# A later branch and an earlier conversion in a fused attention, expert and Fourier-mixing kernel

## The chip, the cores and the metric

The kernel runs on one core of one Trainium2 chip. The metric is the device time of one execution in microseconds (us); smaller is better. The engines are PE (TensorE, matrix products; PEld is its weight load), DVE (VectorE), ACT (ScalarE), POOL (GpSimd) and SP (SyncE, which here only issues DMA transfers).

## What is computed

Three layers follow each other on 4 sequences of 576 rows with 512 channels.

```python
x = attention_with_decay(q, k, v)                  # 8 heads, no softmax
for b, s:                                          # 8 experts, one per row
    e = argmax(logits[b, s]) or the expert of the row before
    out[b, s] = p[e] * (relu(x[b, s] @ w1[e]) @ w2[e])
u  = x + real(fft(fft(x, axis=1), axis=2))         # x: the experts' output
un = (u - mean(u)) / sqrt(var(u) + 1e-06)
y  = u + relu(un @ w_ch1) @ w_ch2                  # 512 -> 2048 -> 512
```

## The kernel before

Every large matrix product is made of three float16 products: each float32 operand is split into a high part (names with `h`) and a low part (names with `l`), and the products are high·high, high·low and low·high. A weight matrix is worked on in pieces of 128x1024. One piece takes the largest absolute value of each partition (`absmax`, L234 on ACT or L236 on DVE), then for a whole matrix one common scale: `peak` (L250 to L255) makes a diagonal matrix `diag` on DVE, `spread` (L260) multiplies it with ones on PE so that each partition sees all maxima, DVE takes the maximum (L261), `scale` (L266, L269) makes the factor `ws`, and `split` makes the high part on ACT (L276) and the low part on DVE (L281).

The channel weights arrive as 64-bit floats. DVE builds the 32-bit floats out of the integer words with five operations for a tile of 128x512: three in `convert_first` (L294, L296, L298), two in `convert_second` (L303, L306). Of the 16 pieces of the two channel matrices (`jobs`), 14 are converted during the experts. The last two, pieces 6 and 7 of the second matrix `w2`, are converted in the channel part by `convert` (L1679), half a piece at a time, and stored to DRAM.

The experts (`moe`) go one after another. For each, `products` (L807) makes the first layer in 8 steps f, ACT and POOL take relu and split (L818, L820, L822), `outputs` makes the second layer (L834, 24 products), ACT scales the result into `y` (L846), and POOL scatters its rows to `x2` in DRAM with an indirect DMA (L848). The last expert has 128 rows; its remaining 160 rows (`late`) and one more group run through `late.hidden`, f = 0 to 3 at the end of `moe` and f = 4 to 7 at the start of `channels`; there the low part `hidl` is made on DVE.

`overflow` holds a loop for experts with more rows than planned. Its branch (L2085, `If(most > 0)`) is met once by every engine and the loop isn't entered with these inputs. In the kernel before, it stands between two hand-ordered schedules: the part of the program ahead of it is arranged by a scheduler, and everything behind it runs in the order in which the code is written. The scheduler mixes nine of the last expert's 24 output products between the steps of its first layer, puts 22 of the 24 products of the late rows' f = 0 and 1 ahead of the branch on PE, and on POOL puts the branch ahead of the scatter.

Behind the branch, `channels` loads the rows of the first of 4 batches from `x2` (`tr.load(0)`, SP, L1191 and L1157), finishes the late rows and makes the Fourier transform of batch 0: `even` and `odd` fold the rows on DVE (L1204 to L1221: tiles `xe`, `xo`, `fee`, `foo`), `twice` adds and subtracts folds (L1227, L1228), `down` is the transform along the rows on PE (L1248, from `fee` and `foo`), `adds` and `sums` put the parts together (L1340, L1343).

Then comes the first channel layer of batch 0, a loop over f = 0 to 15. In each f, PE makes 12 products of 128x512 (L1613, banks `g`, three of them in turn), ACT takes the relu (`gr`, L1809) and a cast (L1810), and DVE the low part (`hd`, L1811). Two generators add one step in each f: `more` (`tr.steps(1)`, from f = 7 on) is the transform of batch 1, and `left` (`rest()`) is the work on weights: it ends the first matrix in f = 0 to 3, converts piece 6 in f = 4 to 7 and piece 7 in f = 8 to 11, and then comes to the common scale (`peak`, `spread`, `scale`) and the splits of the second matrix. Ahead of `down(0)` of batch 1, 22 products whose result isn't used (L1578) are put on PE. The second channel layer (L1827) follows, and then the same for the other batches.

Of the kernel before, what the change touches and what calls it, by code (L numbers as in the profile page):

```python
# [9 lines left out]
FP32 = mybir.dt.float32  # L10
FP16 = mybir.dt.float16
BF16 = mybir.dt.bfloat16
I32 = mybir.dt.int32
# [39 lines left out]
DONE = 14  # L53
# [237 lines left out]

def convert_first(V, r, t):

    V.tensor_scalar(out=t, in0=r[:, :, 1], scalar1=0x7FFFFFFF, scalar2=None, op0=ALU.bitwise_and)  # L294
    f = t.bitcast(FP32)
    V.tensor_scalar(out=f, in0=f, scalar1=TINY, scalar2=None, op0=ALU.max)  # L296

    V.tensor_scalar(out=t, in0=t, scalar1=3, scalar2=0x3FFFFFF8, op0=ALU.logical_shift_left, op1=ALU.bitwise_and)  # L298


def convert_second(V, r, t):

    V.scalar_tensor_tensor(  # L303
        out=t, in0=r[:, :, 1], scalar=-0x40000000, in1=t, op0=ALU.bitwise_and, op1=ALU.bitwise_or
    )
    V.scalar_tensor_tensor(  # L306
        out=t, in0=r[:, :, 0], scalar=29, in1=t, op0=ALU.logical_shift_right, op1=ALU.bitwise_or
    )


class Doubles:
# [13 lines left out]
    def first(self, j):  # L325
        t = self.t[j] = self.pool.tile([128, 1024], I32, tag="d", name="d", bufs=2)
        convert_first(self.nc.vector, self.raw[j], t)
# [533 lines left out]
class Late:  # L861
# [18 lines left out]
    def outputs(self, bank):  # L880
# [15 lines left out]
        first=1.4,  # L896
# [9 lines left out]
        first=0.3,  # L906
        second=3.6,
        store=6.9,
        raw=0.5,
# [58 lines left out]
def moe(octx, tc, nc, A, xs, x2, rows_in, rows_out, pieces, weights, who, conv, low, start, beyond, z, hid0, mt0, wst, small):  # L968
# [82 lines left out]
    def out(w, hid, mt, fs, t, n, do, amid=None):  # L1051
        y = lambda: wk.tile([128, 512], FP32, tag="y", name="y", bufs=3)
        ps = p2.tile([128, 512], FP32, tag="ps2", name="ps2")
        leave = outputs(nc, ps, y, x2, rows_out, w, hid, mt[:, t, 0:1], fs[:, t : t + 1], t, n, amid)
        for job in do:
            job()
        leave()
# [43 lines left out]
    first = [[] for _ in range(8)]  # L1101
# [6 lines left out]
    for e in range(E):  # L1108
        w, n = weights(e), CAPS[e] if e < E - 1 else HEAD
        if e == E - 1:  # L1110
            pieces.more = None
        xt, mt = X.pop(e)
        if e > 0 and e + 1 < E:
            fetch(e + 1)
        tiles = (n + 127) // 128

        todo = halves(weights, conv, 2 * e, 8) if e else first
        hid = wk.tile([128, 2, 8, n], FP16, tag="hid", name="hid", padded_shape=[128, 2, 8, CAP])
        hid = [hid[:, x] for x in range(2)]
        for f in range(8):  # L1120
            ps = p1.tile([128, CAP], FP32, tag="ps1", name="ps1")[:, 0:n]
            products(nc, ps, *w.dst, xt, f)
            for do in todo[f]:
                do()
            if f == 4 and e + 2 < E:
                pad(e + 2)
            r = wk.tile([128, CAP], FP32, tag="r", name="r", bufs=3)[:, 0:n]
            for _ in relu(nc, nc.gpsimd, ps, r, hid, f):
                pass
        fs = factors(w, mt, tiles + (end.n + 127) // 128 if e == E - 1 else tiles)  # L1130
        if e == E - 1:
            end.fs = fs
        for i, m in ((n // 128, n % 128), (tiles + end.n // 128, end.n % 128 if e == E - 1 else 0)):
            if m:

                to, k = mt[:, i, 0:1], 128 // m
                nc.vector.tensor_scalar(out=to, in0=to, scalar1=float(k), scalar2=side[k], op0=ALU.mult, op1=ALU.add)
        if e == E - 1:
            mx.close()
            yield  # L1140
        todo = halves(weights, conv, 2 * e + 1, tiles) if e else [[sizes]]
        for t in range(tiles):

            amid = partial(weights(e + 1).spread, 0, lambda: bank()[:, 0:128]) if e and t == 0 else None
            out(w, hid, mt, fs, t, n, todo[t], amid)
    end.hidden(range(LATE), bank, lambda: wk.tile([128, CAP], FP32, tag="r", name="r", bufs=3))
    ctx.close()
    yield end
# [12 lines left out]
class Transform:  # L1161
# [299 lines left out]
    def place(self, b, i):  # L1461

        t, y = i % 3, i // 3
        k0, n = TL[t]
        p0 = 1 if y and t < 2 else 0
        at = b * S + k0 + (n if y else 0)
        return t, y, p0, n, slice(at, at + n - p0)
# [62 lines left out]
def channels(ctx, tc, nc, A, w1, w2, un, u, out, tr, wst, idn, late, jobs):  # L1530
# [4 lines left out]
    cp = pool(name="gc", bufs=1)  # L1535
# [16 lines left out]
    h1, l1 = w1.dst  # L1552
    h2, l2 = w2.dst
    w2.shared.bank = lambda: p2.tile([128, 512], FP32, tag="g2", name="peak")[:, 0:128]
    tr.load(0)
    nc.sync.dma_start(out=orow, in_=A["orow"])
    turn = [0]
# [12 lines left out]
    some, final = late.outputs(bank)  # L1570
    leave = some()
    z = [bank() for _ in range(5)]
    V = nc.vector

    def still(n, ps):

# [29 lines left out]
    xt = [room().rearrange("p (k n) -> p k n", k=4) for _ in range(2)]  # L1606

    def first(f, ps, xt, steps=range(3)):

        for i in steps:  # L1610
            m, x = ((h1, 0), (l1, 0), (h1, 1))[i]
            for k in range(4):
                nc.tensor.matmul(  # L1613
                    out=ps,
                    lhsT=m[:, k + 4 * (f // 8), 128 * (f % 8) : 128 * (f % 8) + 128],
                    rhs=xt[x][:, k, :],
                    start=(k == 0 and i == 0),
                    stop=(k == 3 and i == 2),
                )

    def weave(*gs):
        gs = list(gs)
        while gs:
            gs = [g for g in gs if next(g, gs) is None]
# [7 lines left out]
    rest = bank()  # L1632
    idle(IDLE[0])
    adds = [tr.add(0, t, *ps[t]) for t in range(3)]
    weave(adds[0])
    tr.sums(0, 0)
    next(adds[1])
    rates = [tr.rate(0, [0]), tr.rate(0, [1, 2])]
    next(rates[0])
# [11 lines left out]
    weave(turns[0])  # L1651
    weave(turns[3])

    half = [[x[:, :, c] for x in xt] for c in (slice(0, 255), slice(255, 512))]
    ahead = [bank() for _ in range(4)]
    ahead = [ahead[i] for i in (0, 3, 1, 2)]
    place = lambda f, c: ahead[f][:, 0:255] if c == 0 else ahead[f][:, 255:512]
    for f in range(3):
        first(f, place(f, 0), half[0], range(2))
    norms = {i: tr.scaled(0, i, e) for i, e in ((1, nc.scalar), (4, V), (2, V))}  # L1660
    turns = [tr.turned(0, i, norms[i], xt, bank()) for i in (1, 4, 2)]
    weave(*turns)
    for f in range(4):
        first(f, place(f, 0), half[0], range(2 if f < 3 else 0, 3))
    for f in range(4):
        first(f, place(f, 1), half[1])

    def last():

# [9 lines left out]

    def convert(j):  # L1680

        V = nc.vector
        t = w2.pieces[j] = wst.tile([128, 1024], FP32, tag="wst", name="wst")
        for i in range(2):
            raw = wst.tile([128, 512, 2], I32, tag="wst", name="raw")
            nc.sync.dma_start(out=raw, in_=jobs[8 + j][0][:, i])
            convert_first(V, raw, t[:, 512 * i : 512 * i + 512].bitcast(I32))
            yield
            convert_second(V, raw, t[:, 512 * i : 512 * i + 512].bitcast(I32))
            yield  # L1690
        w2.absmax(j)
# [121 lines left out]
    for _ in left:  # L1813
        pass
    V.scalar_tensor_tensor(
        out=fs[:, 0:1], in0=w1.inv[:, 0:1], scalar=2.0**-10 / C2, in1=w2.inv[:, 0:1], op0=ALU.mult, op1=ALU.mult
# [6 lines left out]
    for t in range(4):  # L1823
        ps = p2.tile([128, 512], FP32, tag="g2", name="g2")
        for f in range(16):
            for i, (m, x) in enumerate(((h2, 0), (h2, 1), (l2, 0))):
                nc.tensor.matmul(  # L1827
                    out=ps,
# [30 lines left out]
    for r0 in range(512, NT, 256):  # L1859
        xt = X.pop(r0)  # L1860
        xt = xt[:, 0:4], xt[:, 4:8]
        j = (r0 - 512) // 256
# [12 lines left out]
        for f in range(8):  # L1875
# [36 lines left out]
        steps = [  # L1912
            (0, "d2", ((slice(0, 4, 2), 1),)),
            (1, "d1", ((slice(1, 4, 2), 1),)),
            (2, "e1", ((slice(0, 4, 3), 1),)),
            (3, "w22", ((0, 2), (1, 1))),
            (5, "e3", ((0, 1),)),
            (4, "w11", ((2, 1), (3, 2))),
            (6, "e2", ((3, 1),)),
        ]  # L1920
        if j == 0:

            steps = steps[3:6] + steps[2:3] + steps[6:] + steps[:2]
# [12 lines left out]
        def place(i):  # L1936
            q, tag = (p2, "g2") if i % 3 else (p1, "g1")
            return q.tile([128, 512], FP32, tag=tag, name=tag)[:, 0:256]
# [195 lines left out]
def fused_kernel(tc, A, out, stop=None):  # L2134
    nc = tc.nc
    with ExitStack() as ctx:
        xs = tc.dram_tile([(E + 1) * REG, XW], FP16, name="xs")
        x2 = tc.dram_tile([NT, 512], FP32, name="x2")
# [3 lines left out]
        with tc.manual_schedule():  # L2142
            wp = ctx.enter_context(tc.tile_pool(name="wp", bufs=1))
            wst = ctx.enter_context(tc.tile_pool(name="wst", bufs=8))
# [4 lines left out]
            bufs = [  # L2149
                (wp.tile([128, 8, 1024], FP16, name=f"wh{j}"), wp.tile([128, 8, 1024], FP16, name=f"wl{j}"))  # L2150
                for j in range(2)
            ]
# [21 lines left out]
            jobs = []  # L2174
# [72 lines left out]
            idn, n_i, who, low, start, beyond = attention(keep, tc, nc, A, xs, rows_in, hook, beside, after, z, weights(0), bufs[1], hid0, mt0)  # L2247
# [10 lines left out]
            next(steps)  # L2258
            for t, n in zip(tables, ("f_cs", "f_sn", "f_cd", "f_sd")):
                nc.sync.dma_start(out=t.rearrange("p a b -> p (a b)"), in_=A[n])  # L2260
        overflow(tc, nc, A, xs, x2, idn, n_i)
        with tc.manual_schedule():
            late = next(steps)
            c2x.close()
            tr = Transform(ctx, tc, nc, x2, un, u, rows_out, tables)
            channels(ctx, tc, nc, A, c1, c2, un, u, out, tr, wst, idn, late, jobs)
# [46 lines left out]
```

## Time and profile before

| what | value |
|---|---|
| time, median of 3 runs | 809.13 us (806.35 to 814.45) |
| profiled execution, its own time | 809.86 us |
| its span | 808.1 us |
| mean granted TensorE clock | 0.98 of full speed |
| PE busy | 741.5 us, 92% |
| DVE busy | 604.2 us, 75% |
| ACT busy | 418.9 us, 52% |
| POOL busy | 189.6 us, 23% |

The span is the time from the first to the last instruction in the trace; the execution's own time has 1.8 us more. In the timelines each row is a group of equal instructions: start, time from start to the end of the last, engine, line and operation, and in brackets how long the engine had been idle and what released it. A granted clock of 1.00 is TensorE at 2.4 GHz, 0.50 at 1.2 GHz.

### The profile page before, as it was taken

To read this page: it belongs to the slowest core of one execution; us is meant where nothing else is said; L and a number is where in the kernel's file an instruction comes from. 1 tells how busy PE (TensorE), PEld (TensorE's weight loads), DVE (VectorE), ACT (ScalarE), POOL (GpSimd) and SP (SyncE) were. 2 spreads that over 40 slices of the span, in tenths; PEclk is the share of its full clock that TensorE was granted. 3 is DMA by queue.
4 is the path that set the end of the run, shared out by engine and by line. 5 is a ranking of instruction groups with operands and counts; after the bars stand their busy time and mean duration, and the time that the engine had idled before them with its cause. 6 is when DMAs were issued, how large, how long until landed. Compare 5 with 4: busy or idle time off the path is not lost. (4 is left out here: it accounts for less than half of the span.)

```text
span 808.1 us, 17327 instructions
## 1 busy us (share of the span) xinstructions
PE 741.5 (92%) x6571; PEld 552.4 (68%) x6571; DVE 604.2 (75%) x1390; ACT 418.9 (52%) x857; POOL 189.6 (23%) x289
## 2 busy tenths in 40 slices
PE   8898898899899898789998999989889999999996
PEld 5687775546556555566644547868778888888885
DVE  3578988877898898857787986978958495737362
ACT  1356654778788787864744643515423361504140
POOL 3566442544355245322100002010010101010101
PEclk9999999999999999999998999999999999999998
DMA  9998349889899889932256357620380016110000
GB/s 294 348 302 312 108 131 306 226 296 374 312 280 322 319 248 310 351 110 91 84 175 236 127 192 204 188 68 2 112 198 2 27 53 171 53 33 21 27 2 27
DMA packets 91932, 142.30 MB, mean 176 GB/s; under 512 B 48116, under 2 KB 49017, under 8 KB 90814
## 3 DMA queue, kind: packets, MB, share of 16 engines
q1 hardware_dynamic: 87246, 126.78, 48.9%
q0 software_dynamic: 4592, 14.31, 4.6%
q8 instruction: 54, 0.88, 0.4%
q14 instruction: 40, 0.33, 0.1%
HBM read 97.55 MB, written 35.12 MB: 164 GB/s over the span
## 5 line engine op out<-in xcount | busy, mean ns | idle before, releaser
L1613 PE MATMUL g<-gxt,wh 128*128 128x256 f16 (+1 forms) x992 | 143.5, 285 | 3.6 <-DMA gxt<-un 3.4
L1927 PEld LDWEIGHTS <-hd 128*128 128x128 f16 x1176 | 114.7, 98 | 26.6 <-issue 6.4
L1613 PEld LDWEIGHTS <-wh 128*128 128x128 f16 x1056 | 103.1, 98 | 29.7 <-issue 8.4
L281 DVE SCALAR_TENSOR_TENSOR wl<-wst,ws,wh 128x1024 f16<-128x1024 f32 (+1 forms) x82 | 102.9, 1288 | 20.4 <-ACT wh L276 20.1
L1787 POOL DMA_INDIRECT out<-u,orow x18 | 19.1, 1064 | 391.2 <-DVE u L1956 293.3
L276 ACT ACTIVATE wh<-wst,ws 128x1024 f16<-128x1024 f32 x80 | 88.8, 1141 | 35.5 <-DVE ws L269 35.5
L807 PE MATMUL ps<-xt,wh 128*128 128x320 f16 (+4 forms) x544 | 81.3, 292 | 6.6 <-DMA xt<-xs 3.6
L807 PEld LDWEIGHTS <-wh 128*128 128x128 f16 x640 | 59.4, 103 | 38.7 <-issue 20.8
L834 PE MATMUL ps<-wh,hid 128*128 128x512 f16 (+2 forms) x528 | 84.2, 302 | 0.5 <-POOL hid L822 0.5
L1927 PE MATMUL g<-wh,hd 128*128 128x256 f16 x448 | 78.3, 273 | 2.9 <-DVE s L1898 1.6
L1613 PE MATMUL g<-gxt,wl 128*128 128x256 f16 (+1 forms) x496 | 80.5, 285 | 0.0
L1898 DVE SCALAR_TENSOR_TENSOR s<-g,r 128x256 f32<-128x256 f32 x168 | 53.1, 370 | 31.3 <-ACT hd L1892 30.5
L834 PEld LDWEIGHTS <-hid 128*128 128x128 f16 (+2 forms) x792 | 46.3, 100 | 42.5 <-issue 2.5
L822 POOL TENSOR_TENSOR hid<-r,hid 128x320 f16<-128x320 f32 (+3 forms) x64 | 64.0, 1011 | 41.4 <-ACT hid L820 40.8
L1956 DVE SCALAR_TENSOR_TENSOR u<-g,ffs,u 128x256 f32<-128x256 f32 (+1 forms) x63 | 34.1, 567 | 49.3 <-PE g L1927 48.7
L1891 ACT ACTIVATE r<-g 128x256 f32<-128x256 f32 x56 | 21.2, 379 | 92.8 <-PE g L1613 86.8
L1927 PE MATMUL g<-e,hd 128*128 128x256 f16 x504 | 61.2, 276 | 5.4 <-DVE u L1956 4.4
L1871 ACT ACTIVATE hd<-s 128x640 f16<-128x640 f32 x56 | 41.3, 737 | 46.8 <-DVE s L1898 46.8
L1927 PE MATMUL g<-wl,hd 128*128 128x256 f16 x224 | 61.1, 273 | 0.0
L1613 PEld LDWEIGHTS <-wl 128*128 128x128 f16 x528 | 51.8, 98 | 11.8 <-issue 1.1
L234 ACT ACTIVATE wh<-wst 128x1024 bf16<-128x1024 f32 x51 | 53.5, 1050 | 9.1 <-DMA wst<-in_moe_w 5.1
L834 PE MATMUL ps<-wl,hid 128*128 128x512 f16 (+2 forms) x264 | 56.3, 302 | 0.0
(303 smaller groups left out, 1352.3 us busy)
## 6 DMA issues: line engine op xcount, KB each, us to landing
wst<-in_moe_w SPq DMA_DIRECT2D x64, 512.0 KB
raw<-in_ch SPq DMA_DIRECT2D x14, 1024.0 KB
qk<-in_qkv SPq DMA_DIRECT2D x18, 512.0 KB
vk<-in_qkv SPq DMA_DIRECT2D x16, 512.0 KB
pair<-ch SPq DMA_DIRECT2D x32, 256.0 KB
ch<-d SPq DMA_DIRECT2D x14, 512.0 KB
wst<-ch SPq DMA_DIRECT2D x14, 512.0 KB
u<-u SPq DMA_DIRECT2D x9, 512.0 KB
```

Source lines behind the costliest of these rows:

```text
L234: self.nc.scalar.activation(out=x, in_=t, func=ACTF.Abs, accum_out=self.am[:, j : j + 1])
L276: self.nc.scalar.activation(out=self.dst[0][:, j, :], in_=self.pieces[j], func=ACTF.Copy, scale=self.by(j))
L281: self.nc.vector.scalar_tensor_tensor(out=l[:, j, c], in0=self.pieces[j][:, c], scalar=self.by(j), in1=h[:, j, c], op0=ALU.mult, op1=ALU.s ...
L807: nc.tensor.matmul(out=ps, lhsT=m[:, k, 128 * f : 128 * f + 128], rhs=xt[:, x + k, :], start=(k == 0 and i == 0), stop=(k == 3 and i == 2),)
L822: e.tensor_tensor(out=l[:, f, :], in0=r, in1=h[:, f, :], op=ALU.subtract)
L834: nc.tensor.matmul(out=ps[r * j : r * j + r, 0:d], lhsT=hid[x][:, f, 128 * t : 128 * t + r], rhs=m[:, 4 + f // 2, c : c + d], start=(f == ...
L1613: nc.tensor.matmul(out=ps, lhsT=m[:, k + 4 * (f // 8), 128 * (f % 8) : 128 * (f % 8) + 128], rhs=xt[x][:, k, :], start=(k == 0 and i == 0) ...
L1871: nc.scalar.activation(out=hd[:, 0, 2:7], in_=s, func=ACTF.Copy, scale=C2 / 2)
L1891: nc.scalar.activation(out=r, in_=p[:, 1:3], func=ACTF.Relu)
L1898: V.scalar_tensor_tensor(out=d, in0=x, scalar=0.0, in1=y, op0=ALU.max, op1=op)
L1927: nc.tensor.matmul(out=ps, lhsT=hid[k][:, y, x, :], rhs=E[w][m][k], start=(k == 0 and m == y == 0), stop=(k == 7 and y == 1),)
L1956: V.scalar_tensor_tensor(out=y, in0=p, scalar=fs[:, c : c + 1], in1=y, op0=ALU.mult, op1=ALU.add)
```

## The change

There are two edits. The first puts a `yield` into `moe` behind the loop over the last expert's output tiles, and the branch of `overflow` there, inside the hand-ordered schedule: the last expert's products and scatter stand ahead of it, all of the late rows' products behind it. The second takes piece 6 of the second matrix out of the loop: its two halves are loaded right behind the branch (`raws`), ahead of the rows of batch 0. Half 0 is converted behind the low parts of the late rows' f = 0 to 3. Half 1 is converted around `adds[0]` of batch 0's transform. `convert(6)` then only takes `absmax`.

```diff
@@ moe
             out(w, hid, mt, fs, t, n, todo[t], amid)
+    yield
     end.hidden(range(LATE), bank, ...)
@@ channels
+    first_t = wst.tile([128, 1024], FP32, tag="wst", name="wst")
+    raws = [cp.tile([128, 512, 2], I32, tag="gxt", name="raw", bufs=2) for _ in range(2)]
+    for i in range(2):
+        nc.sync.dma_start(out=raws[i], in_=jobs[DONE][0][:, i])
+    half = lambda i: (V, raws[i], first_t[:, 512 * i : 512 * i + 512].bitcast(I32))
+    V = nc.vector
+    convert_first(*half(0))
+    convert_second(*half(0))
     tr.load(0)
@@
     adds = [tr.add(0, t, *ps[t]) for t in range(3)]
+    convert_first(*half(1))
     weave(adds[0])
     tr.sums(0, 0)
+    convert_second(*half(1))
@@ convert(j)
+        if j == DONE - 8:
+            w2.pieces[j] = first_t
+            w2.absmax(j)
+            return
@@ fused_kernel
-        overflow(tc, nc, A, xs, x2, idn, n_i)
-        with tc.manual_schedule():
+            next(steps)
+            overflow(tc, nc, A, xs, x2, idn, n_i)
             late = next(steps)
```

On SP, behind the branch, this stood before (`fxy` holds the rows of batch 0, `x_58` is `x2`):

```order
L2085 UNCONDITIONAL_BRANCH x2
L1191 DMA fxy_6438<-x_58 128x512
L1157 DMA fxy_6438<-x_58 112x512
L1157 DMA fxy_6438<-x_58 15x512
L1191 DMA fxy_6439<-x_58 128x512
```

And this stands there now:

```order
L2098 UNCONDITIONAL_BRANCH
L1559 DMA raw<-in_ch 128x1024 x2
L1192 DMA fxy_6435<-x_58 128x512
L1158 DMA fxy_6435<-x_58 112x512
L1158 DMA fxy_6435<-x_58 15x512
L1192 DMA fxy_6436<-x_58 128x512
```

Two loads of half a piece each have come ahead of the first load of rows.

On DVE, in the loop over f, this stood before around the common scale of the second matrix (`hd` at the top is that of f = 12):

```order
L303 SCALAR_TENSOR_TENSOR wst<-raw,wst 128x512
L306 SCALAR_TENSOR_TENSOR wst<-raw,wst 128x512
L1811 TENSOR_TENSOR hd<-gr,hd 128x512
L236 TENSOR_REDUCE am<-wst 128x1
L250 TENSOR_REDUCE wm<-am 128x1
L251 TENSOR_SCALAR wm<-wm 128x1
L255 TENSOR_SCALAR diag<-idn,wm 128x128
L1811 TENSOR_TENSOR hd<-gr,hd 128x512
L261 TENSOR_REDUCE wg<-peak 128x1
```

And this stands there now (the folds at the top are those of batch 1's first 128 rows, which follow `hd` of f = 7; `hd` at the end is that of f = 8):

```order
L1211 TENSOR_TENSOR fee_6438<-xe 128x128
L1218 TENSOR_TENSOR xo<-fxy_6435 128x512
L1220 TENSOR_TENSOR xo<-xo 128x255
L1221 TENSOR_TENSOR foo_6442<-xo 128x127
L1222 TENSOR_TENSOR foo_6442<-xo 128x128
L236 TENSOR_REDUCE am<-wst 128x1
L250 TENSOR_REDUCE wm<-am 128x1
L251 TENSOR_SCALAR wm<-wm 128x1
L255 TENSOR_SCALAR diag<-idn,wm 128x128
L1824 TENSOR_TENSOR hd<-gr,hd 128x512
```

The common scale has moved four steps of f ahead, to right behind the first folds of batch 1, with no conversion ahead of it any more but that of piece 7.

On PE, this stood before around `spread` (the products of the two `g` banks belong to f = 13 and 14):

```order
L1613 MATMUL g_7371<-gxt,wh_75 128x512
L1248 MATMUL zps<-f_cs,fee_6444 128x145
L1248 MATMUL zps<-f_cs,fee_6442 128x145
L1248 MATMUL zps<-f_cs,fee_6443 128x290
L260 LDWEIGHTS onesb
L260 MATMUL peak<-diag,onesb 128x128
L1613 LDWEIGHTS wh_75
L1613 MATMUL g_7404<-gxt,wh_75 128x512
```

And this stands there now (the banks are those of f = 9 and 10):

```order
L1621 MATMUL g_7245<-gxt,wh_75 128x512
L260 LDWEIGHTS onesb
L260 MATMUL peak<-diag,onesb 128x128
L1621 LDWEIGHTS wh_75
L1621 MATMUL g_7282<-gxt,wh_75 128x512
```

The product of `spread` now stands between the first layer's steps f = 9 and f = 10, ahead of every `down` of batch 1.

## Rows read from the trace of the kernel before

**Rows 1.** Timeline of PE: start, us, engine, line, operation, tiles, count [idle before].
```profile
352.35 0.96 PE L807 MATMUL ps<-xt,wh 128*128 128x160 f16 x6 [2.94 <-PEq L2085]
...
359.04 0.38 PE L834 MATMUL bank<-wh,hidh 128*128 128x512 f16 x1
```

**Rows 2.** Instructions of the branch, L2085: count, shortest/median/longest in ns, first start.
```profile
L2085 PEldq COMPARE_BRANCH  x1: 3352/3352/3352, 348.6 to 348.6; - x1
```

**Rows 3.** Timeline of ACT, POOL and SP from the last scatter on.
```profile
348.51 0.67 ACT L846 ACTIVATE y<-ps,fs 128x512 f32<-128x512 f32 x1
...
350.91 0.99 POOL L848 DMA_INDIRECT x<-y,mt  x1 [5.26 <-issue]
...
355.30 0.34 SPq L1191 DMA_DIRECT2D fxy<-x  x1
```

**Rows 4.** Timeline of DVE from the late rows to the sums of batch 0.
```profile
359.93 0.32 DVE L822 TENSOR_TENSOR hidl<-r,hidh 128x160 f16<-128x160 f32 x1 [0.51 <-ACT hidh L820]
360.18 0.69 DVE L1204 TENSOR_TENSOR xe<-fxy 128x512 f32<-128x512 f32 x1
...
375.08 0.42 DVE L1340 TENSOR_TENSOR fxy<-fxy,bank 128x256 f32<-128x256 f32 x1 [2.19 <-ACT own L1338]
...
378.63 0.42 DVE L1340 TENSOR_TENSOR fxy<-fxy,bank 128x256 f32<-128x256 f32 x1 [1.84 <-ACT own L1338]
```

**Rows 5.** Timeline of PE in the transform of batch 0.
```profile
369.22 1.04 PE L1248 MATMUL bank<-f_sn,foo 128*128 128x145 f32 x4 [0.25 <-DVE foo L1227]
```

**Rows 6.** Timeline of SP and DVE: a conversion in the loop, as it was.
```profile
401.31 0.83 SPq L1686 DMA_DIRECT2D raw<-in_ch  x2
...
405.72 0.43 DVE L294 TENSOR_SCALAR wst<-raw 128x512 int32<-128x512 int32 x1 [1.85 <-DMA raw<-in_ch]
...
407.59 0.68 DVE L303 SCALAR_TENSOR_TENSOR wst<-raw,wst 128x512 int32<-128x512 int32 x1
```

**Rows 7.** Windows: us, busy PE PEld DVE ACT POOL, granted clock, DMA share, GB/s.
```profile
357.00:357.50 0.50, 0.50 (x10) 0.50 (x8) 0.06 (x1) 0.38 (x2) 0.00 (x0) 1.00 0.98 373
```

**Rows 8.** Timeline of PE in the loop over f.
```profile
403.00 1.89 PE L1613 MATMUL g<-gxt,wh 128*128 128x512 f16 x8
...
419.69 4.91 PE L1578 MATMUL zps<-wh 128*128 128x512 f16 x22
427.58 2.30 PE L1248 MATMUL zps<-f_cs,fee 128*128 128x145 f32 x6 [2.98 <-DVE fee L1227]
429.68 1.91 PE L1613 MATMUL g<-gxt,wh 128*128 128x512 f16 x4
...
434.49 1.15 PE L1248 MATMUL zps<-f_cs,fee 128*128 128x145 f32 x6
```

**Rows 9.** Timeline of DVE in the loop over f.
```profile
412.71 0.68 DVE L1811 TENSOR_TENSOR hd<-gr,hd 128x512 f16<-128x512 f32 x1
...
416.49 0.42 DVE L294 TENSOR_SCALAR wst<-raw 128x512 int32<-128x512 int32 x1
...
430.63 1.21 DVE L236 TENSOR_REDUCE am<-wst 128x1 f32<-128x1024 f32 x1
...
432.26 0.29 DVE L255 TENSOR_SCALAR diag<-idn,wm 128x128 bf16<-128x128 f32 x1
...
435.73 0.29 DVE L261 TENSOR_REDUCE wg<-peak 128x1 f32<-128x128 f32 x1 [2.58 <-PE peak L260]
```

**Rows 10.** Timeline of ACT in the loop over f.
```profile
412.83 1.06 ACT L234 ACTIVATE wh<-wst 128x1024 bf16<-128x1024 f32 x1 [3.81 <-DVE wst L306]
...
436.44 2.19 ACT L276 ACTIVATE wh<-wst,ws 128x1024 f16<-128x1024 f32 x2 [0.31 <-DVE ws L269]
438.53 0.58 ACT L1809 ACTIVATE gr<-g 128x512 f32<-128x512 f32 x1
```

**Rows 11.** Window behind PE's idle in the loop (columns as in rows 7).
```profile
433.50:434.50 1.00, 1.00 (x5) 0.51 (x4) 0.00 (x0) 0.00 (x0) 0.00 (x0) 0.67 0.94 307
```

**Rows 12.** Timeline of PE at a later idle.
```profile
592.50 0.60 PE L1613 MATMUL g<-gxt,wh 128*128 128x256 f16 x4 [3.03 <-DMA gxt<-un]
```

More of the change, by code (lines that the diff above doesn't have):

```diff
@@ L1572, in channels @@
     z = [bank() for _ in range(5)]
-    V = nc.vector
     def still(n, ps):
@@ L1652, in channels @@
     weave(turns[3])
-    half = [[x[:, :, c] for x in xt] for c in (slice(0, 255), slice(255, 512))]
+    parts_of = [[x[:, :, c] for x in xt] for c in (slice(0, 255), slice(255, 512))]
     ahead = [bank() for _ in range(4)]
@@ L1658, in channels @@
     for f in range(3):
-        first(f, place(f, 0), half[0], range(2))
+        first(f, place(f, 0), parts_of[0], range(2))
     norms = {i: tr.scaled(0, i, e) for i, e in ((1, nc.scalar), (4, V), (2, V))}
@@ L1663, in channels @@
     for f in range(4):
-        first(f, place(f, 0), half[0], range(2 if f < 3 else 0, 3))
+        first(f, place(f, 0), parts_of[0], range(2 if f < 3 else 0, 3))
     for f in range(4):
-        first(f, place(f, 1), half[1])
+        first(f, place(f, 1), parts_of[1])
     def last():
@@ L1680, in convert @@
     def convert(j):
-        V = nc.vector
+        if j == DONE - 8:
+            w2.pieces[j] = first_t
+            w2.absmax(j)
+            return
         t = w2.pieces[j] = wst.tile([128, 1024], FP32, tag="wst", name="wst")
```

## The prediction

> **What bounds the kernel now.** I read the page's busy shares first: PE works for 92% of the span, so time is lost or won where PE stands idle or at the low clock, and only there. The timeline of PE shows two such places beside the edits. At the branch it idles 2.94 us [rows 1], and the branch instruction itself lasts 3352 ns [rows 2]. In the loop over f it idles 2.98 us ahead of `down(0)` of batch 1, waiting for DVE's `fee` [rows 8]; behind that the granted clock is 0.67 as late as 433.5 to 434.5 [rows 11], and the same six `down` products take 2.30 us there against 1.15 us at 434.49 [rows 8]. The timeline of DVE says what PE waits for: from `xe` at 360.18 [rows 4] DVE folds batch 0 with hardly a gap, and PE follows it in idles such as 0.25 us for `foo` [rows 5]. In the loop DVE carries the conversions, the folds and `hd` one behind the other. So both edits are judged by DVE's queue, and by what PE's order makes of it.
>
> **The branch and the scatter.** The same products, relus and one scatter are issued, in another order. On POOL the scatter starts at 350.91, 1.73 us behind `y`, which ends at 349.18 (348.51 + 0.67) [rows 3], since the branch's instructions stand ahead of it. Now it stands ahead of them. But `y` itself moves back a little, as nine of its 24 products no longer fill gaps of the first layer; I put `y` at +0.1 to +0.8 and the scatter at 350.2 to 351.0, and take 350.5. SP issues the first load of rows 4.4 us behind the scatter's start (355.30 - 350.91) [rows 3]; its first transfer is then possible at 354.9. On PE, 22 products that stood ahead of the branch come behind it. Before, 74 products took from 352.35 to 359.04, 6.7 us [rows 1], part of it at half speed. 96 products from a start between 349.7 and 352 end at 356.4 to 359.8. This is near 359.04, and PE isn't what the folds wait for, so I count nothing. Were DVE not in the way, this end could cost 0.8 us or win 2.6 us.
>
> **The two new loads and half 0.** SP's first transfers are now the two halves of piece 6, 0.52 MB each, and the rows come two issues later, each 0.42 us (0.83 for two) [rows 6]: 355.7 for 354.9, against 355.30 before. DVE can't begin `xe` until half 0 is converted, since its five operations stand ahead of the last four `hidl` in program order. They cost three times 0.43 and twice 0.68, 2.65 us [rows 6]. When does half 0 land? The row nearest to it is the loop's own load: issued at 401.31, used at 405.72, 4.4 us, with other transfers under way [rows 6]. At the rate of a full queue, 373 GB/s [rows 7], 0.52 MB take 1.4 us behind a start of about 1 us, 2.5 us in all. The queues are nearly empty here, so I take the lower end: landed at 357.4, converted at 360.1, four `hidl` of 0.32 [rows 4] to 361.4, `xe` at 361.5 instead of 360.18: +1.3 us. The upper end is 359.3 and +3.1. The low end is +0.3, if the data lands at 356.4, about when DVE is done with the first four `hidl`.
>
> The Trainium skill (DMA: Bandwidth & Descriptors, the table of two cost components) gives a transfer about 2.0 us fixed plus its bytes over 436 GB/s, as an estimate 3.2 us here. By it half 0 would land at 358.1 and the term would be +2.0; rows 6 alone, with its 4.4 us, stands above it.
>
> **Half 1.** Three operations (1.3 us) go ahead of `adds[0]` and two (1.4 us) behind `sums(0,0)`. DVE idles 2.19 and 1.84 us in just these two places, ending at 375.08 and 378.63, while ACT works on `own` [rows 4]. These idles cover them; without the cover half 1 would cost 2.65 us. I count nothing.
>
> **The loop over f.** The edit takes 5.3 us of conversion off DVE. But the order shows where the time goes: `rest()` runs one step in each f, and with `convert(6)` reduced to `absmax`, everything behind it comes four steps earlier, the common scale too. Nothing else on DVE ahead of f = 8 becomes shorter, because piece 7's conversion now stands in f = 4 to 7 where piece 6's stood. ACT takes `absmax` of piece 6 at f = 4, 1.06 us [rows 10], ahead of the relu of f = 4; PE loses about 1 us of its lead in f = 7. The row at 403.00 holds the last four products of f = 6 and the first four of f = 7; twelve products of 0.216 us (22 take 4.75 and the tail of the last) make 2.59 us a step, so f = 7 began at 403.86 and f = 9 now ends at 403.86 + 1.0 + 3 x 2.59 = 412.6 on the old scale [rows 8]. Its next product is `spread`, and that needs `diag`. On DVE, `hd` of f = 7 ends at 413.4 (412.71 + 0.68), the folds of batch 1's first rows run until 416.49, and then come L236 to `diag`, which took from 430.63 to 432.55, 1.92 us [rows 9]: 418.4. PE stands idle for 5.8 us where it did not before.
>
> From there: `hd` of f = 8 to 418.9, the second folds (3.2 us, as the first) to 422.1, L261, L266 and L269 to 422.8 [rows 9]. ACT then makes the high parts of two pieces, 2.19 us, ahead of the relu of f = 9 with 0.58 [rows 10]: 425.6. PE makes f = 10 and 11 from 418.45, 5.2 us at full clock, but f = 12 needs the bank of f = 9, so not before 425.65. Then 2.6 us for f = 12, 4.75 us for the 22 filler products [rows 8], 0.95 us for `down(0)` (1.15 with the tail), whose `fee` I put at 432.7, behind the folds of the last 66 rows, two more low parts and two `hd`, so that its idle of 2.98 us is gone, and 2.6 us for f = 13: `down(1)` at 436.55. Before it stood at 434.49 [rows 8]: **+2.05 us**. This holds if the low clock behind the idle costs no more than the 2.0 us by which f = 11 ends ahead of the bank. If it costs what it cost behind 427.58 (1.15 us for `down` and 2.2 us for f = 13, whose twelve products take from 429.68 to 434.49 instead of 2.59), f = 12 starts at 427.0 and `down(1)` at 437.9: +3.4. Behind it, f = 13 to 15 have only `hd` on DVE, and PE was dense there anyway, so nothing comes back. If ACT and PE come out of f = 8 with more lead than I give them, the idle is longer and its end the same.
>
> The Trainium skill (TensorE: Matmul & The Clock Gate, Part 1) says that an idle PE falls back to half its rate. By rows 11 it did so here after 2.98 us; by that rule the 5.8 us would leave the low clock behind them too, and the sum would be the larger one, +4.7, if that stretch is as long as the one that rows 8 shows.
>
> **The sum.** +1.3 for half 0 and +2.05 for the early scale: +3.35. The profiled execution is 809.86 us with a span of 808.1; it becomes 813.2. The median of the three runs is 0.7 lower, so I predict **812.5 us**. The bounds of the two terms (+0.3 to +3.1, +2.05 to +3.4) give 811.5 to 815.6, on the median. Runs of before lie between 806.35 and 814.45.
>
> **The rivals.** *The loop wins what it gives up* (faster). If `diag` is ready before PE ends f = 9, at 412.6, there is no new idle, while the idle of 2.98 and the low clock behind it (3.3 us) are gone: -6.3 + 1.3, 804.1 us. DVE would have to be 5.8 us earlier. For it speaks that 5.3 us of DVE work has left the loop; against it that this work left from behind f = 8, and `diag` stands behind a full piece of conversion and a fold. It decides at the start of L236: 410.7 or before. Were the branch's idle and its half speed shortened too, 801 is as far as it goes.
>
> *The loads hold up the front and the clock stays low* (slower). Half 0 takes 4.4 us as in the loop, +3.1, the rows behind two loads of 0.52 MB come later still, and PE is at half clock for as long as behind 427.58, +3.4: +6.5, 815.6 us. For it speak rows 6 and rows 11; against it that the queues are nearly empty at 355.
>
> *The delay is swallowed later.* PE has idles behind the loop, such as 3.03 us at 592.50 for a load of `gxt` [rows 12]. If what they wait for were issued by an engine with slack, a delay of 3 us would shorten them: 809 to 810 us. Against it: that load follows DVE work which follows PE's own products, so it comes later with them.
>
> **How the numbers follow.** The forecast (811 to 814) has 0.5, the slow front and clock 0.2, the swallowed delay 0.2, the win in the loop 0.1. The range of 8 in 10 reaches from the runs near the swallowed delay, 806.5, to the slow case with the runs' scatter, 818.5; about 0.1 lies on either side. A measurement of this kernel can tell about 1% from no change, that is 801.0 and 817.2. Faster than that asks for the win in the loop and a gain at the branch: 0.06. Slower asks for the slow case and more: 0.14. Within 1%: 0.80.
>
> **What would show it.** Right: PE idle for about 6 us ahead of the product of `spread`, released by `diag`; no idle ahead of `down(0)` of batch 1; L294 of half 0 released by the load of `raw`; `xe` at about 361.5; the scatter before 351. Wrong: `diag` on DVE earlier than PE's end of f = 9, a `raw` that lands before the fourth `hidl`, or later idles of PE that shrink by as much as the loop lost.

## The result, and the profile after

The changed kernel takes 818.21 us (median of 10 runs, 815.03 to 819.38); the kernel before, run beside it, 812.09 us (10 runs, 806.35 to 814.65; the three runs shown ahead of the prediction are among them). The ratio is 1.0069, 95% interval 1.0045 to 1.0092: **slower by 0.7%**, some 5.6 us by the ratio and 6.1 by the medians. A second measurement, of 4 runs, gave 1.0118 (1.0084 to 1.0152) with a median of 821.12. The first median lies within the range of 806.5 to 818.5, 0.3 us below its upper end; the second lies above it. The size that was predicted, 3.35 us, was too small.

The profiled execution has a span of 816.9 us for 808.1. The first view is the timeline of PE of the changed kernel, from the branch to the second channel layer.

```profile
350.37 0.44 PE L807 MATMUL ps<-xt,wh 128*128 128x160 f16 x4 [1.26 <-PEq L2098]
...
367.69 1.47 PE L1249 MATMUL bank<-f_cs,fee 128*128 128x145 f32 x8 [1.74 <-DVE fee L1228]
370.47 3.14 PE L1249 MATMUL bank<-f_cs,fee 66*128 66x290 f32 x10 [1.31 <-DVE fee L1210]
...
426.22 0.29 PE L260 MATMUL peak<-diag,onesb 128*128 128x128 bf16 x1 [6.35 <-DVE diag L255]
426.30 1.92 PE L1621 MATMUL g<-gxt,wh 128*128 128x512 f16 x4
...
435.87 4.91 PE L1586 MATMUL zps<-wh 128*128 128x512 f16 x22
440.62 1.15 PE L1249 MATMUL zps<-f_cs,fee 128*128 128x145 f32 x6
...
444.19 1.15 PE L1249 MATMUL zps<-f_cs,fee 128*128 128x145 f32 x6
```

Three things answer to [rows 1, 8]. The idle at the branch is 1.26 us instead of 2.94. The idle of 2.98 ahead of `down(0)` of batch 1 is gone, the six products take 1.15 us and not 2.30. But the product of `spread` waits 6.35 us for its diagonal, and there are two new idles in batch 0's transform, 1.74 and 1.31 us, in which PE waits for DVE's folds (`fee`).

The timelines of DVE, POOL and SP of the changed kernel answer to [rows 3, 4]:

```profile
350.31 1.50 POOL L848 DMA_INDIRECT x<-y,mt  x1 [4.39 <-ACT y L846]
354.17 1.77 SPq L1559 DMA_DIRECT2D raw<-in_ch  x2
356.25 0.33 SPq L1192 DMA_DIRECT2D fxy<-x  x1
...
358.58 0.43 DVE L294 TENSOR_SCALAR wst<-raw 128x512 int32<-128x512 int32 x1 [2.89 <-DMA raw<-in_ch]
...
361.31 0.79 DVE L822 TENSOR_TENSOR hidl<-r,hidh 128x160 f16<-128x160 f32 x3
362.41 0.33 DVE L822 TENSOR_TENSOR hidl<-r,hidh 128x160 f16<-128x160 f32 x1 [0.31 <-ACT hidh L820]
363.90 0.69 DVE L1205 TENSOR_TENSOR xe<-fxy 128x512 f32<-128x512 f32 x1 [1.17 <-DMA orow<-in_orow]
...
382.37 0.42 DVE L1341 TENSOR_TENSOR fxy<-fxy,bank 128x256 f32<-128x256 f32 x1 [4.64 <-ACT own L1339]
```

The scatter is earlier, half 0 is converted from 358.58 on, and the folds start at 363.90 instead of 360.18. DVE is through with half 0 and the low parts at 362.74 and then waits 1.17 us for a load (the profile names `orow`, a small load issued right behind the rows; in a second profile the idle is 0.41 us and the load is that of the rows). The transform then takes longer than it did: `adds` starts 18.5 us behind the folds, where it was 14.9 [rows 4]. The windows of the changed kernel show why (us, busy time of PE, PEld, DVE, ACT and POOL, granted clock, DMA share, GB/s):

```profile
366.00:376.00 10.00, 7.00 (x27) 4.73 (x28) 9.52 (x25) 2.65 (x10) 1.06 (x2) 0.76 0.39 145
376.00:386.00 10.00, 10.00 (x65) 9.52 (x63) 4.64 (x13) 3.22 (x11) 1.27 (x1) 0.73 0.16 54
```

In the kernel before, in a second profile of it (the ratio of its runs to the others of this kernel was 0.9988, 0.9956 to 1.0019), the same windows read

```profile
366.00:376.00 10.00, 9.63 (x62) 6.89 (x60) 8.05 (x22) 3.09 (x12) 1.06 (x2) 1.00 0.29 99
376.00:386.00 10.00, 8.90 (x156) 7.45 (x155) 6.79 (x25) 6.43 (x19) 4.68 (x4) 1.00 0.01 2
```

PE worked through batch 0's transform at 2.4 GHz before; now, from 371.2 on, 0.7 us behind the second idle, it stands at 1.2 GHz until 381.

To compare profiles, the span is cut where the same work begins. The time up to the end of `y` of the last expert varies between profiles by several us (348.2 to 355.1) and is left out. "y" is that end, "folds" the start of the first `xe`, "f = 4" the first 128x512 product of the channel layer's loop, "second layer" the first product of L1827 or what it became. All are read from the timelines, in us.

| profile | y to folds | folds to f = 4 | f = 4 to second layer | rest | y to end |
|---|---|---|---|---|---|
| before | 11.0 | 35.9 | 46.3 | 365.7 | 458.9 |
| before, second profile | 11.3 | 35.7 | 45.5 | 364.6 | 457.2 |
| changed | 13.9 | 39.5 | 48.7 | 364.8 | 466.9 |
| changed, second profile | 12.9 | 39.3 | 49.2 | 365.3 | 466.7 |
| branch alone | 10.1 | 40.0 | 45.2 | 364.7 | 460.0 |
| conversion alone | 13.7 | 37.8 | 48.7 | 365.0 | 465.2 |
| late scale | 13.7 | 39.1 | 41.0 | 365.5 | 459.3 |
| fill | 14.9 | 35.8 | 48.6 | 363.9 | 463.1 |
| late scale and fill | 12.9 | 35.8 | 41.1 | 365.3 | 455.0 |
| rows first | 10.0 | 38.8 | 40.7 | 364.8 | 454.2 |
| half 0 later | 12.8 | 40.5 | 49.5 | 365.6 | 468.3 |
| one half | 10.6 | 36.5 | 45.8 | 364.3 | 457.2 |
| half 1 at f = 1 | 10.7 | 36.6 | 41.0 | 364.3 | 452.6 |
| the same, old branch | 11.1 | 37.7 | 40.8 | 365.1 | 454.7 |

The change costs 2.2 us up to the folds (13.4 for 11.2, means of two profiles each), 3.6 in batch 0's transform (39.4 for 35.8), 3.1 in the loop (49.0 for 45.9), and nothing behind it. That is 8.7 us in the profiles; the two ratios give 5.6 and 9.6.

### The profile page after: what moved, and what is told of

It reads as the page before. It is cut to its first block, busy times and chain, and to the rows that moved or that the text cites. A ratio compares the mean times of both kernels' runs of the same rounds, so it can differ in the third digit from the quotient of the medians.

```text
span 816.9 us, 17330 instructions
## 1 busy us (share of the span) xinstructions
PE 743.2 (91%) x6571; PEld 553.7 (68%) x6571; DVE 605.7 (74%) x1390; ACT 419.3 (51%) x857; POOL 191.5 (23%) x289
## 5 line engine op out<-in xcount | busy, mean ns | idle before, releaser
L1969 DVE SCALAR_TENSOR_TENSOR u<-g,ffs,u 128x256 f32<-128x256 f32 (+1 forms) x63 | 34.1, 569 | 49.3 <-PE g L1940 48.7
```

The costliest lines, as they stand in the source:

```text
L1969: V.scalar_tensor_tensor(out=y, in0=p, scalar=fs[:, c : c + 1], in1=y, op0=ALU.mult, op1=ALU.add)
```

## The experiments

**Each edit alone.** Branch alone is the kernel before with the `yield` and the branch moved:

```diff
+    yield
     end.hidden(range(LATE), bank, ...)
...
-        overflow(tc, nc, A, xs, x2, idn, n_i)
-        with tc.manual_schedule():
+            next(steps)
+            overflow(tc, nc, A, xs, x2, idn, n_i)
             late = next(steps)
```

> The kernel before with the first edit alone: the branch behind the last expert's scatter, no conversion moved. My theory, that the front's loss comes from the two new loads and half 0 on DVE: DVE starts the folds of batch 0 (the first L1204) within 1 us of the 360.2 us of before, f = 4 of the first channel layer starts within 1.5 us of 396.1, and the time is 0 to 2 us below the kernel before. Rival, that the later release of ACT and DVE from the branch (352.9 and 353.7 us in the changed kernel against 351.5 and 353.4) makes the front late by itself: folds at 361.5 or later, f = 4 2 us or more behind 396.1, time 2 to 4 us above before.

Conversion alone is the changed kernel with these lines taken back.

> The kernel before with the second edit alone: the early conversion of piece 6, the branch in its old place. My theory: the whole loss is here. Folds of batch 0 start 3 us late or more, PE falls to 1.2 GHz in batch 0's transform and loses about 3.5 us more, and the product of the early scale waits about 6 us for its diagonal, which costs 2 to 2.5 us net: 7 to 9 us above before in the span, as in the changed kernel's profile. Rival, that the two edits need each other for the loss: no more than 4 us above before.

The branch alone made no difference that can be told: ratio 1.0012 (0.9986 to 1.0038). The conversion alone made all of the first measurement's loss: 1.0075 (1.0047 to 1.0103), 6.1 us, so the rival that the two edits need each other is out; its front and its loop take as long as those of the changed kernel. But the branch alone isn't quiet inside. The late rows' low parts are done 8.5 us behind `y` and not 11.1, yet the folds gain only 1 us, since now they wait for their rows; and then the transform takes 40.0 us, against my expectation of no loss there. DVE waits once more, 1.30 us, for the second rows, and this is part of the 4.2 us that the transform has grown by. The timelines of DVE and PE of that kernel:

```profile
363.29 0.69 DVE L1205 TENSOR_TENSOR xe<-fxy 128x512 f32<-128x512 f32 x1 [1.60 <-DMA fxy<-x]
366.27 0.69 DVE L1205 TENSOR_TENSOR xe<-fxy 128x512 f32<-128x512 f32 x1 [1.30 <-DMA fxy<-x]
...
368.48 1.47 PE L1249 MATMUL bank<-f_cs,fee 128*128 128x145 f32 x8 [0.94 <-DVE fee L1228]
371.26 1.13 PE L1249 MATMUL bank<-f_cs,fee 66*128 66x290 f32 x5 [1.31 <-DVE fee L1210]
```

Here too two idles of about 1 us stand in the transform, and the clock falls behind them, to 0.50 from 374 to 380. In the conversion alone it does so from 372 to 378. So each edit alone brings the low clock into the transform, from opposite sides. With the branch alone PE is through with the late rows and the unused products behind them 14.3 us after `y`, and with the kernel before 16.9 and 17.3 us: PE is early. With the conversion alone it is 17.1, and the folds are 2.5 us late. Either way PE then waits for DVE. The rival for the branch, that its release makes the folds late, is wrong when counted from `y`; that it makes f = 4 late is right, by another way.

**The scale back at its old steps.** Four empty steps are put ahead of the common scale:

```diff
+        for _ in range(4):
+            yield
         w2.peak(0)
```

> The changed kernel with four empty steps ahead of the common scale of the second matrix, so that the scale and its product stand at f = 12 and 13 as before. My theory, that the early scale costs PE a wait of 6.35 us and gives back only the idle ahead of the transform's first product: that wait is gone, nothing takes its place because DVE has 5.3 us less to do ahead of the transform's sums, and the second channel layer starts 6 to 8 us earlier than in the changed kernel, time 6 to 8 us below it (810 to 812). Rival, that the wait only moves to the transform's first product of batch 1 as it stood before: 2 to 3 us below the changed kernel. Rival, that the work of the scale then delays the second layer: no gain.

The changed kernel was measured a second time beside it.

> The changed kernel once more, for a second profile beside two of the kernel before. If the low clock in batch 0's transform belongs to the change, the folds to f = 4 take 39 us or more again at 1.2 GHz in part; if it comes by chance, they may take 36. y to the folds 13 to 14 us, f = 4 to the second layer 48.7 us.

The late scale brings the ratio to 1.0008 (0.9988 to 1.0027); the changed kernel's were 1.0069 and 1.0118. The loop from f = 4 on takes 41.0 us, 8 us less than the changed kernel's and 4.9 less than that of before, so both rivals, a gain of 2 to 3 us and no gain, are out. The timeline of PE of this kernel shows no wait at either place:

```profile
428.00 4.91 PE L1586 MATMUL zps<-wh 128*128 128x512 f16 x22
433.05 1.47 PE L1249 MATMUL zps<-f_cs,fee 128*128 128x145 f32 x6
...
437.94 0.22 PE L260 MATMUL peak<-diag,onesb 128*128 128x128 bf16 x1
```

So with the whole of piece 6 gone the loop wins 4.9 us, near the 5.3 us of work that left it; the early scale took this away and 3 us more. The second profile of the changed kernel repeats the first:

```profile
424.82 0.29 PE L260 MATMUL peak<-diag,onesb 128*128 128x128 bf16 x1 [5.93 <-DVE diag L255]
```

The transform stands at the low clock again (granted 0.65 and 0.84 in the two windows from 366 to 386). The wait and the low clock are in both profiles of the changed kernel and in neither of the kernel before, so they belong to the change.

**Unused products in the transform.** These fill PE's two new idles (the row "fill" of the table):

```diff
-STILL = 8, 22, 16
+STILL = 16, 22, 16
...
     tr.even(0, 2)
+    still(6, z[3])
```

> The changed kernel with 8 more unused products ahead of batch 0's first transform product and 6 more ahead of its third part, where PE idled 1.74 and 1.31 us. My theory, that these idles bring PE to 1.2 GHz from 371 to 381 us and that this costs 3.5 us: the granted clock stays at 1.00 there, f = 4 starts 3 to 4 us before the 403.4 us of the changed kernel, time 3 to 4 us below it. Rival, that the clock falls whatever PE does in these idles: f = 4 within 0.5 us of 403.4 or later, no gain.

The ratio is 1.0036 (1.0016 to 1.0056), about 2.7 us under the first measurement of the changed kernel. The windows of this kernel:

```profile
366.00:376.00 10.00, 8.05 (x39) 3.80 (x37) 9.31 (x26) 2.83 (x8) 1.10 (x2) 1.00 0.54 188
376.00:386.00 10.00, 9.66 (x149) 9.10 (x152) 8.09 (x21) 4.00 (x14) 2.54 (x2) 1.00 0.17 54
```

The clock stays at 1.00 and folds to f = 4 takes 35.8 us, as before, although the folds started later in this profile than in any other (14.9 us behind `y`) and one idle of 1.64 us was left ahead of the first product. f = 4 itself was only 1.5 us earlier than in the changed kernel's profile, and 2.7 us when counted from `y`, because of that late start; 3 to 4 us had been expected. The rival is out: what PE does in these idles decides the clock. In all six profiles with these products the clock stays at 1.00 here, and in all six profiles of changed kernels without them it falls. Half 1 is hidden at the full clock as well: behind its operations DVE still idles ahead of both sums:

```profile
380.89 0.42 DVE L1341 TENSOR_TENSOR fxy<-fxy,bank 128x256 f32<-128x256 f32 x1 [0.93 <-ACT own L1339]
...
384.43 0.42 DVE L1341 TENSOR_TENSOR fxy<-fxy,bank 128x256 f32<-128x256 f32 x1 [0.54 <-ACT own L1339]
```

**Both cures, and the loads.** Late scale and fill together:

> The changed kernel with both cures so far: the common scale at its old steps, and the unused products in batch 0's transform. Times of stages, from the traces so far: last expert's y to the folds 13.8 us as in the changed kernel (before: 11.0), folds to f = 4 35.8 (before 35.9, changed 39.5), f = 4 to the second transform product of batch 1 33.1 (before 38.4, changed 40.8). My theory, that the three losses are separate and add: about 2.7 us below before. Rival, that a stage that becomes shorter only makes a later wait longer: 0 to 1 us below before.

0.9963 (0.9939 to 0.9987): 3.0 us below before, as the sum of separate losses says. What is left of the loss is the front. Two runs ask whether the queues or DVE hold the folds up. One leaves the loads ahead of the rows and converts half 0 later:

```diff
-    convert_first(*half(0))
-    convert_second(*half(0))
...
-    convert_first(*half(1))
+    for i in range(2):
+        convert_first(*half(i))
     weave(adds[0])
     tr.sums(0, 0)
-    convert_second(*half(1))
+    for i in range(2):
+        convert_second(*half(i))
```

> The changed kernel with its loads where they are, ahead of the rows, but with half 0 converted behind the transform's folds, together with half 1. This tells the queues from DVE. If the 1 MB of loads ahead of the rows holds them up, the folds still start 13.0 to 14.5 us behind y, released by a load of rows. If half 0 on DVE does it, they start 10 to 11.5 us behind y.

The other has the same conversion, late scale and fill, and issues the two loads behind those of the rows:

> As the run before, but the two halves of piece 6 are loaded behind the rows of batch 0, and both halves are converted around adds[0] and sums(0,0). My theory, that the rows are held up by the 1 MB ahead of them in the queues and by half 0 on DVE: y to folds 10 to 11 us, folds to f = 4 36 to 37.5 (5.3 us of conversion in idles of 4.0), f = 4 to the second transform product 33, together 3.5 to 5.5 us below before. Rival, that the conversion in the sums' idles costs its full 2.65 us more or that the loads come too late for it: no better than 2.7 us below before.

With half 0 later the timelines of SP and DVE read

```profile
357.37 1.81 SPq L1192 DMA_DIRECT2D fxy<-x  x1
...
359.87 0.32 DVE L822 TENSOR_TENSOR hidl<-r,hidh 128x160 f16<-128x160 f32 x1 [0.50 <-ACT hidh L820]
...
364.56 0.69 DVE L1205 TENSOR_TENSOR xe<-fxy 128x512 f32<-128x512 f32 x1 [4.37 <-DMA fxy<-x]
```

DVE is free 4.37 us before the rows are there, and the folds start 12.8 us behind `y`, about as late as in the changed kernel (13.9 and 12.9) and far from the 10 to 11.5 that would have spoken for DVE. With the rows first they start at 10.0:

```profile
360.78 0.34 SPq L1192 DMA_DIRECT2D fxy<-x  x1
...
365.09 0.69 DVE L1205 TENSOR_TENSOR xe<-fxy 128x512 f32<-128x512 f32 x1 [1.48 <-DMA fxy<-x]
```

From the issue of the first rows to the folds it is 7.19 us in the first of these kernels and 4.31 us in the second. So the 1 MB ahead of the rows holds them up by itself, and half 0 on DVE stands mostly in the shade of that wait. Half 0 later came out at 1.0133 (1.007 to 1.0195, from two runs), the slowest of all: its rows come late, and it has the low clock, the early scale, and both halves between the sums. Rows first came to 0.9939 (0.9913 to 0.9966), 5.0 us below before, but folds to f = 4 takes 38.8 us, where I had expected 36 to 37.5. The five operations of the two halves, 5.3 us, are more than the idles of 2.19 and 1.84 us in [rows 4] hold, and PE waits for the sums:

```profile
386.89 0.24 PE L834 MATMUL bank<-wh,hidh 128*32 128x128 f16 x4 [2.07 <-DVE fxy L1341]
```

Another 1.02 us goes to a wait of DVE for the second rows.

**Where the halves can hide.** One half leaves half 1 in the loop at f = 4 and 5:

> As the run with the rows loaded first, but only half 0 of piece 6 is converted early, around adds[0] and sums(0,0), where DVE's idles of 2.19 and 1.84 us can hide 2.65; half 1 stays in the loop (f = 4 and 5), the scale at f = 12. My theory, that the 2.8 us which the run with both halves lost between the folds and f = 4 are the part of 5.3 us that finds no idle: folds to f = 4 36 us (38.75 with both halves), f = 4 to the second layer 41 to 42 us, y to the folds 10 us: 1 to 2 us below the run with both halves, 6 to 7 us below before. Rival, that any conversion between the sums costs its time: folds to f = 4 37.5 us or more, no gain.

Half of this expectation held. Folds to f = 4 took 36.5 us, so one half does fit between the sums. The loop took 45.8 and not 41 to 42; the ratio, 0.9967 (0.9944 to 0.9991), is no gain over both halves. Its timelines of ACT and PE:

```profile
408.54 1.06 ACT L234 ACTIVATE wh<-wst 128x1024 bf16<-128x1024 f32 x1 [4.03 <-DVE wst L306]
...
410.23 1.02 PE L1619 MATMUL g<-gxt,wh 128*128 128x512 f16 x4 [1.88 <-ACT gr L1821]
...
427.54 1.47 PE L1249 MATMUL zps<-f_cs,fee 128*128 128x145 f32 x6 [2.05 <-DVE fee L1228]
```

With half of the conversion left in, the idle ahead of `down(0)` is back at 2.05 us. And ACT's `absmax` of piece 6 waits 4.03 us for the half that is still converted in the loop, with the relus in the queue behind it, so that PE waits 1.88 us for `gr`. These two idles of 3.9 us stand against 2.98 before and one of 0.64 with the late scale. So the loop's gain isn't in proportion to the work taken out. It seems to come only when DVE gets ahead of PE at `down(0)`, and here it didn't. The next run puts half 1 into f = 1 and 2, where DVE waits for ACT's high parts, with its raw words in buffers that stand free until the loop's end. The last is the same with the branch at its old place.

```diff
-    raws = [cp.tile([128, 512, 2], I32, tag="gxt", name="raw", bufs=2) for _ in range(2)]
+    raws = [cp.tile([128, 512, 2], I32, tag="pair", name="raw", bufs=2) for _ in range(2)]
...
         for j in range(4, 8):
             w1.split(j)
+            if j in (5, 6):
+                (convert_first if j == 5 else convert_second)(*half(1))
             yield
```

> Rows first, scale at f = 12, the unused products, half 0 around adds[0] and sums(0,0) as in the run with one half, but half 1 in f = 1 and 2 of the loop, where the first matrix's splits leave DVE waiting for ACT; its raw words wait in buffers that are first used behind the loop. My theory, that an early conversion is free where DVE has an idle of its own and that the loop's gain asks for all 5.3 us to be gone ahead of f = 4: folds to f = 4 36 to 36.5 us, f = 4 to the second layer 41 to 42, together 5 to 6 us below before, 1 us below the run with both halves between the sums. Rival, that DVE's lead in f = 1 and 2 is needed: f = 4 to the second layer 43 us or more, no better than 4 us below before.

> The same with the branch in its old place, ahead of the last expert's scatter on POOL. With the branch alone at the new place the folds started 1.0 us earlier behind y, but waited for their rows, and the time stayed the same. If the new place is worth something when PE is kept busy, this is 0.5 to 1.5 us slower than the run beside it, with y to folds 11.0 us for 10 to 10.5. Rival, that it is worth nothing: within 0.5 us.

Half 1 at f = 1 has 36.6 and 41.0 us in its two stages and a ratio of 0.9932 (0.9907 to 0.9958): 806.53 us where the kernel before has 811.39 beside it, faster than both kernels. The theory's numbers held: 36 to 36.5, 41 to 42, and 5 to 6 us below before. With the old branch the ratio is 0.9939 (0.9916 to 0.9962), 0.75 us more in the medians, while its profile is 2.1 us longer from `y` on; the intervals overlap, so the worth of the branch's new place is not settled. It isn't a clean test of the branch either: with the old branch PE reaches the unused products ahead of the transform 15.2 us behind `y` and not 12.3, has no idle left in it, and DVE waits 2.84 us ahead of the first sums (0.93 beside it), so the unused products seem to push the transform back (37.7 us for 36.6). The old branch with fewer unused products was not run. In the kernel with the old branch the timeline of PE shows the old wait, and the products behind it at the low clock again (0.96 us, as in [rows 1]):

```profile
354.85 0.96 PE L807 MATMUL ps<-xt,wh 128*128 128x160 f16 x6 [3.19 <-PEq L2100]
```

## Why the prediction was right, and where it was too small

The direction and the place in the loop were right, the size was not: 3.35 us were predicted, and 5.6 to 9.6 measured. That the first median fell into the range is luck in part. The range's upper end was made of a late half 0, a long low clock in the loop and the scatter of the runs, and the largest loss, in batch 0's transform, is none of these.

- **The scatter** started at 350.31, within 350.2 to 351.0, 0.27 us behind `y` and not 1.73. PE's idle at the branch shrank to 1.26 us. The branch alone changes the time by nothing that can be told, as counted, but not because it does nothing. The prediction priced what PE could win at this end at 2.6 us, and with the branch alone PE does come to the transform that much earlier (14.3 us behind `y` for 16.9 and 17.3). It then waits there, and its clock falls.
- **The front, +1.3 predicted, +2.2 measured** from `y` on. Two steps failed. The first is that the rows would only come "two issues later": they share the queues with 1 MB, and the run with half 0 later shows that this alone makes the folds about as late as they are. In the prediction DVE's conversion ended last ahead of the folds, and in the trace a load does. The second is "I take the lower end": half 0 was there 4.4 us behind its issue (358.58 - 354.17; 4.2 in the second profile), as the loop's own load was in [rows 6], and not in 2.5. The Trainium skill (DMA: Bandwidth & Descriptors, the table of two cost components) gives 3.2 us by estimate for 0.52 MB, from a fit to transfers that POOL issues and not SP; the trace is above it, with two loads under way together. The queues were nearly empty at 355, as said, but I had looked at what was in them and not at what the change puts there.
- **Half 1** was covered, as counted. In the changed kernel 4.64 us of idle are left behind its first three operations, since PE was slow, and at the full clock 0.93 and 0.54 us are left; the transform then takes 35.8 us as before. Both halves there cost about 2.9 us (rows first, 38.8 for 35.9 us), of which 1.02 is the wait for the second rows.
- **Batch 0's transform, nothing predicted, +3.6 measured.** This is the term that is missing. The prediction said that PE follows DVE there in idles of 0.25 us [rows 5] and then moved the folds without asking how long those idles become. The folds came 2.2 us later behind `y` and PE came 1.3 us earlier (means of two profiles each), so they became 1.74 and 1.31 us, and the clock fell to 1.2 GHz from 371 to 381. The fill brings the whole 3.6 back with the folds still late, so all of it is the clock's. The price of the low clock was weighed in the loop alone.
- **The loop, +2.05 predicted, +3.1 measured** (2.4 between the first two profiles). The wait at `spread` was put at 5.8 us and is 6.35 and 5.93. Its end is as described: the first products behind it run slow (1.92 us for four), until some 3 us behind the wait in the first profile and nearly 6 in the second, and `down(0)` doesn't wait.
- **The rivals.** "The loop wins what it gives up" is what the kernel with the late scale does: 4.9 us less than before in the loop. The condition on `diag` that was given for it was the right one to look at. "The delay is swallowed later" is out: the rest takes 364.8 and 365.3 us, before 365.7 and 364.6. The slow rival had the first of its two causes, the loads; its second, a low clock of 10 us, came in the transform and not in the loop.

## What to carry to other kernels

When work is taken out of a list that is dealt out one item to a step, everything behind it moves ahead as well; look at the items that another engine waits for, and keep their steps with empty ones. A load placed ahead of others holds them up by the time of its bytes, here some 3 us for 1 MB, and not only by its issue. And an idle that grows on PE has to be priced for the clock behind it too: here two idles of 1.74 and 1.31 us cost 3.6 us by the clock alone. Unused products in the gaps took that price away, though not the wait for DVE itself.

## What was not expected of the hardware

Each engine pays for the branch on its own. In the changed kernel PE is through it after an idle of 1.26 us, but ACT's first relu and DVE's first low part behind it come at 352.98 and 353.77; these are the rows of ACT and DVE:

```profile
352.98 0.30 ACT L818 ACTIVATE r<-ps 128x160 f32<-128x160 f32 x1 [2.95 <-ACTq L2098]
...
353.77 0.79 DVE L822 TENSOR_TENSOR hidl<-r,hidh 128x160 f16<-128x160 f32 x2 [2.84 <-DVEq L2098]
```

The relu and the low part of PE's early products had to wait for this. And the clock doesn't fall behind every idle of the same length: in the first profile of before the products behind the branch's idle of 2.94 us ran at half speed, in the second, behind 2.98 us, they did not, and idles of 3.27 and 3.19 us at the same place, in the conversion alone and in the last kernel of the table, brought half speed again. The row of the second profile:

```profile
354.07 0.58 PE L807 MATMUL ps<-xt,wh 128*128 128x160 f16 x6 [2.98 <-PEq L2085]
```

On the other side, two idles of 1.74 and 1.31 us with work between them brought it down. The Trainium skill (TensorE: Matmul & The Clock Gate, A second HAM failure mode: psum-queue depth-cycling) tells of a kernel in which frequent short idles of PE between groups of products make the clock go back and forth; the transform of the changed kernel agrees, with the clock at 0.50 from 372 to 381. Why one idle of 3 us does it and the next one does not is left open by these runs.
